# A linear-attention scan and a squared-ReLU FFN in one kernel: pairs of chunks, two tokens per partition, and an issue order written by hand

## The chip, the cores and the metric

One core of one Trainium2 chip. The metric is device microseconds of one launch, from the runtime's own clock; it runs about 2 us longer than the span of the profile, which goes from the first to the last instruction. A run is called slow when it is more than 1.5% above the fastest run of the same kernel.

Engines: PE is TensorE, PEld its weight loads, DVE VectorE, ACT ScalarE, POOL GpSimd, SP SyncE. A name with q behind it is that engine's instruction queue where it waits or issues a DMA.

## The reference

Four batches, 8 heads, 768 tokens, head size 32, state size 16. A selective scan with a scalar decay per head and token, in chunks, feeds a two-layer FFN over all 3072 tokens. In condensed form:

```python
cum = np.cumsum(log_a, axis=-1)                       # within a chunk
M = einsum('bhin,bhjn->bhij', C, B) * exp(cum_i - cum_j) * causal
y = einsum('bhij,bhjd->bhid', M, x) + einsum('bhin,bhnd->bhid', C, state) * exp(cum)
state = exp(sum(log_a)) * state + sum_j B_j x_j * exp(cum_last - cum_j)
...
x = y.transpose(0, 2, 1, 3).reshape(3072, 256)
h = np.maximum(x @ w_in, 0.0)                         # 256 -> 2048
out = h * h @ w_out                                   # 2048 -> 256
```

The reference uses chunks of 32 tokens. The length changes the order of the sums and not the result, so both kernels use 128.

## The kernel before

A unit is one batch and one chunk: 24 units. Each has transposes, two groups of four score matmuls, eight 128-column masks, the output and the state. The FFN works on blocks of 512 tokens. The issue order is left to a scheduler, and the score tiles and the FFN's first layer take buffers from one PSUM pool of four (`ps4`).

```python
        for hg in range(2):
            mtq = []
            for q in range(4):
                mt0 = ps4.tile([128, 128], FP32, tag="acc", padded_shape=[128, 512], ...)
                ...
                nc.tensor.matmul(mt0, lhsT, rhs, start=True, stop=True, tile_position=(32 * q, 0))
                mtq.append(mt0)
            mts4 = u_pool.tile([128, 512], BF16, tag="mts4")
            for q in range(4):
                nc.vector.tensor_tensor(out=mts4[:, q * 128:(q + 1) * 128], in0=mtq[q],
                                        in1=mask4[:, 0:128], op=ALU.mult)
...
        for f in range(4 * qi, 4 * qi + 4):               # FFN, a quarter of a 512-token block
            hps = ps4.tile([128, 512], FP32, tag="acc", name=f"hps_{f}")
            for kt in range(2):
                nc.tensor.matmul(hps, w_in_bf[kt][:, f * 128:(f + 1) * 128],
                                 T[:, kt, tb * 512:(tb + 1) * 512], start=(kt == 0), stop=(kt == 1))
            ...
            nc.scalar.activation(out=hbf, in_=hps, func=AF.Relu)
            nc.vector.tensor_tensor(out=h2t, in0=hbf, in1=hbf, op=ALU.mult)
...
        for k in range(2):                                # weights: 3 DMAs from SyncE
            nc.sync.dma_start(out=w_in_f[k], in_=moe_w_in[k * 128:(k + 1) * 128, :])
            nc.scalar.copy(out=w_in_bf[k], in_=w_in_f[k])
```

Of the kernel before, what the change touches and what calls it, by code (L numbers as in the profile page):

```python
# [10 lines left out]
FP32 = mybir.dt.float32  # L12
# [5 lines left out]
def _free_ap(base: bass.AP, offset_elems: int, free_dims):  # L18
    ap0 = list(base.ap)[0]
    return bass.AP(tensor=base.tensor, offset=base.offset + offset_elems,  # L20
                   ap=[list(ap0)] + [list(d) for d in free_dims])


@with_exitstack
def kernel(
# [9 lines left out]
):  # L35
    nc = tc.nc
    NB, NH, S, D = 4, 8, 768, 32
    NST = 16
    L = 128
    NC = S // L  # L40
    NTOK = NB * S

    const_pool = ctx.enter_context(tc.tile_pool(name="const", bufs=1))
    prep_pool = ctx.enter_context(tc.tile_pool(name="prep", bufs=1))
    w_pool = ctx.enter_context(tc.tile_pool(name="w", bufs=1))
    big_pool = ctx.enter_context(tc.tile_pool(name="big", bufs=1))
    bc_pool = ctx.enter_context(tc.tile_pool(name="bc", bufs=3))
    u_pool = ctx.enter_context(tc.tile_pool(name="u", bufs=2))
    st_pool = ctx.enter_context(tc.tile_pool(name="st", bufs=2))
    f_pool = ctx.enter_context(tc.tile_pool(name="f", bufs=2))  # L50
    h2_pool = ctx.enter_context(tc.tile_pool(name="h2", bufs=2))

    eye_bf_np = np.eye(128, dtype=np.float32).astype(ml_dtypes.bfloat16)
    triu_np = np.triu(np.ones((128, 128), dtype=np.float32))
    stril_np = (np.arange(128)[:, None] > np.arange(128)[None, :]).astype(np.float32)
    ones_np = np.ones((128, 128), dtype=np.float32)
    m = (np.arange(128)[:, None] <= np.arange(128)[None, :]).astype(np.float32)
    mask4_np = np.tile(m, (1, 4)).astype(ml_dtypes.bfloat16)

    eye_bf_d = nc.inline_tensor(eye_bf_np, name="eye_bf")  # L60
    eye32_d = nc.inline_tensor(np.eye(32, dtype=np.float32), name="eye32_f")
    dec_d = nc.inline_tensor(np.concatenate([triu_np, stril_np, ones_np], axis=1), name="dec_f32")
    mask4_d = nc.inline_tensor(mask4_np, name="mask4_bf")

    eye_bf = const_pool.tile([128, 128], BF16)
    eye32_f = const_pool.tile([32, 32], FP32)
    dec = const_pool.tile([128, 3, 128], FP32)
    mask4 = const_pool.tile([128, 512], BF16)
    zrow = const_pool.tile([1, 128], BF16)
    nc.sync.dma_start(out=eye_bf, in_=eye_bf_d.ap())  # L70
    nc.sync.dma_start(out=eye32_f, in_=eye32_d.ap())
    nc.sync.dma_start(out=dec, in_=dec_d.ap().rearrange("p (t c) -> p t c", t=3))
    nc.sync.dma_start(out=mask4, in_=mask4_d.ap())
    nc.vector.memset(zrow, 0.0)

    w_in_bf = [w_pool.tile([128, 2048], BF16, name=f"w_in_bf{k}") for k in range(2)]
    w_out_bf = w_pool.tile([128, 16 * 256], BF16)

    T = big_pool.tile([128, 2, NTOK], BF16)

    P_sb = prep_pool.tile([128, 192], FP32)
    Pinv_sb = prep_pool.tile([128, 192], FP32)
    Qrev_sb = prep_pool.tile([128, 192], FP32)
    plast_bd = prep_pool.tile([128, 48], FP32)

    with tc.tile_pool(name="prep2", bufs=1) as prep2, \
         tc.tile_pool(name="ps_prep", bufs=1, space=bass.MemoryType.PSUM) as ps_prep:
        a_nat = prep2.tile([32, S], FP32)
        la_nat = prep2.tile([32, S], FP32)
        la_T = prep2.tile([128, 192], FP32)  # L90
        nc.sync.dma_start(out=a_nat, in_=a.rearrange("b h s -> (b h) s"))
        nc.scalar.activation(out=la_nat, in_=a_nat, func=AF.Ln)
        for cc in range(NC):
            latr = ps_prep.tile([128, 32], FP32, name=f"latr{cc}", tag="latr", padded_shape=[128, 512])
            nc.tensor.transpose(latr, la_nat[:, cc * 128:(cc + 1) * 128], eye32_f)
            nc.vector.tensor_copy(out=la_T[:, cc * 32:(cc + 1) * 32], in_=latr)
        dps = [ps_prep.tile([128, 192], FP32, name=f"dps{t}", tag=f"dps{t}", padded_shape=[128, 512]) for t in range(3)]
        for t in range(3):
            nc.tensor.matmul(dps[t], dec[:, t, :], la_T, start=True, stop=True)
        nc.scalar.activation(out=P_sb, in_=dps[0], func=AF.Exp)  # L100
        nc.scalar.activation(out=Pinv_sb, in_=dps[0], func=AF.Exp, scale=-1.0)
        nc.scalar.activation(out=Qrev_sb, in_=dps[1], func=AF.Exp)
        ptot = prep2.tile([128, 192], FP32)
        nc.scalar.activation(out=ptot, in_=dps[2], func=AF.Exp)
        for q in range(4):
            src = _free_ap(ptot[32 * q:32 * (q + 1), 0:1], q, [[8, 4], [4, 2], [32, 6]])
            nc.vector.tensor_copy(
                out=plast_bd[32 * q:32 * (q + 1), :].rearrange("p (b g c) -> p b g c", b=4, g=2),
                in_=src)

    ps4 = ctx.enter_context(tc.tile_pool(name="ps4", bufs=4, space=bass.MemoryType.PSUM))
    ps_a = ctx.enter_context(tc.tile_pool(name="ps_a", bufs=1, space=bass.MemoryType.PSUM))

    def pad_cols(t):
        return _free_ap(t[:, 0:1], NST, [[32, 8], [1, NST]])

    state_prev = {}
    sps_g = ps_a.tile([128, 128], FP32, tag="sprime", padded_shape=[128, 512], name="sps_g")
    nc.tensor.matmul(sps_g, zrow, zrow, start=True, stop=True, skip_group_check=True)

    pref = {}

    def prefetch(u):
        if u >= NB * NC:
            return
        b, c = u // NC, u % NC
        x_nat = bc_pool.tile([128, 8, 32], FP32, tag="x_nat")
        B_nat = bc_pool.tile([128, 8, NST], FP32, tag="B_nat")
        C_nat = bc_pool.tile([128, 8, NST], FP32, tag="C_nat")
        sl = slice(c * 128, (c + 1) * 128)  # L130
        nc.sync.dma_start(out=x_nat, in_=x[b][:, sl, :].transpose([1, 0, 2]))  # L131
        nc.sync.dma_start(out=B_nat, in_=B[b][:, sl, :].transpose([1, 0, 2]))  # L132
        nc.sync.dma_start(out=C_nat, in_=C[b][:, sl, :].transpose([1, 0, 2]))  # L133
        pref[u] = (x_nat, B_nat, C_nat)

    def ssd_unit(b, c):
        u = b * NC + c
        col0 = c * 32 + b * 8
        x_nat, B_nat, C_nat = pref.pop(u)
        prefetch(u + 3)  # L140
        x4 = bc_pool.tile([128, 8, 32], BF16, tag="x4")
        nc.gpsimd.tensor_copy(out=x4, in_=x_nat)  # L142
        BPinv = bc_pool.tile([128, 256], BF16, tag="BPinv")
        CP = bc_pool.tile([128, 256], BF16, tag="CP")
        Bds = bc_pool.tile([128, 8, NST], BF16, tag="Bds")
        nc.gpsimd.memset(pad_cols(BPinv), 0.0)  # L146
        nc.gpsimd.memset(pad_cols(CP), 0.0)
        pinv_b = _free_ap(Pinv_sb[:, col0:col0 + 1], 0, [[1, 8], [0, NST]])
        p_b = _free_ap(P_sb[:, col0:col0 + 1], 0, [[1, 8], [0, NST]])
        qrev_b = _free_ap(Qrev_sb[:, col0:col0 + 1], 0, [[1, 8], [0, NST]])  # L150
        out_strided_B = _free_ap(BPinv[:, 0:1], 0, [[32, 8], [1, NST]])
        out_strided_C = _free_ap(CP[:, 0:1], 0, [[32, 8], [1, NST]])
        nc.gpsimd.tensor_tensor(out=out_strided_B, in0=B_nat, in1=pinv_b, op=ALU.mult)  # L153
        nc.gpsimd.tensor_tensor(out=out_strided_C, in0=C_nat, in1=p_b, op=ALU.mult)  # L154
        nc.vector.tensor_tensor(out=Bds, in0=B_nat, in1=qrev_b, op=ALU.mult)
        bct_ps = ps_a.tile([128, 512], BF16, tag="bct", padded_shape=[128, 1024])
        for gi, src_t in enumerate((BPinv, CP)):
            for hg in range(2):
                nc.tensor.transpose(bct_ps[:, (gi * 2 + hg) * 128:(gi * 2 + hg + 1) * 128],  # L159
                                    src_t[:, hg * 128:(hg + 1) * 128], eye_bf)  # L160
        bct = bc_pool.tile([128, 512], BF16, tag="bct_sb")
        nc.vector.tensor_copy(out=bct, in_=bct_ps)  # L162
        ypsum = ps_a.tile([128, 2, 128], FP32, tag="ypsum", padded_shape=[128, 2, 256])
        mts = {}
        for hg in range(2):
            mtq = []
            for q in range(4):
# [68 lines left out]
    for u0 in range(3):  # L236
        prefetch(u0)
# [10 lines left out]
    for tb in range(6):  # L248
        for qi in range(4):
            items.append(("q", tb, qi))  # L250
# [54 lines left out]
```

## Time and profile before

| | before |
|---|---|
| time, median of 3 runs | 200.64 us |
| span of the profiled run, granted TensorE clock | 197.0 us, 0.99 |
| TensorE busy | 86% of the span |
| first FFN matmul | 34.95 us |
| a block of 512 tokens, in the full part | 27.7 us |

The prediction below shows the busy row, the tenths and the timeline. Three rows of the costliest groups complete it. Their columns: line, engine, operation, output and inputs, shapes, count; then busy time and the mean ns of one; then the engine's idle time ahead of them and what ended most of it.

```profile
L219 ACT ACTIVATE hbf<-hps 128x512 bf16<-128x512 f32 x96 | 53.6, 596 | 25.9 <-PE hps L214 18.8
L175 DVE TENSOR_TENSOR mts<-mt,mask 128x128 bf16<-128x128 f32 x192 | 47.8, 286 | 26.6 <-PE mt L171 23.4
L171 PE MATMUL mt<-bct 32*128 32x128 bf16 x192 | 29.5, 233 | 2.6 <-ACT hbf L219 1.1
```

ACT and DVE wait for TensorE far longer (18.8 and 23.4 us) than TensorE waits ahead of the scores (2.6 us). TensorE's own stream of many small, separate groups is the limit.

### The profile page before, as it was taken

What the parts mean: (1) busy time and instruction counts of PE and PEld (TensorE: products, weight loads), DVE (VectorE), ACT (ScalarE), POOL (GpSimd) and SP (SyncE); (2) the same over time, 40 slices, a digit from 0 to 9 for tenths busy, and PEclk for the clock granted to TensorE, in tenths of its full rate; (3) what the DMA queues carried; (4) which work ended last, traced back from release to release, by engine and by line L of the source; (5) the groups of instructions that cost most, each with busy time, mean ns of one, the idle gap of its engine ahead of it and who ended that gap; (6) DMA issues with size and microseconds to landing.
All of it is one profiled execution on the core that took longest, in us unless ns stands there. A gap on an engine that the chain in (4) does not pass through costs nothing.

```text
span 197.0 us, 3713 instructions
## 1 busy us (share of the span) xinstructions
PE 169.6 (86%) x1290; PEld 92.9 (47%) x1301; DVE 113.5 (58%) x387; ACT 82.6 (42%) x154; POOL 37.3 (19%) x124
## 2 busy tenths in 40 slices
PE   0356667899999999999999999999999999889883
PEld 0243233344575444564445764446754446633462
DVE  0155657586656768538858367775568674346600
ACT  2420734638222836223664216291137452238710
POOL 2151125421233110215112050213230000000000
PEclk9999999999999999999999999999999999979999
DMA  4978997963156313248320637130400001100011
GB/s 111 116 106 318 370 218 83 114 74 40 26 103 104 44 13 40 47 91 114 42 34 1 105 84 79 13 45 27 93 32 0 0 0 44 57 9 0 3 53 53
DMA packets 81233, 14.32 MB, mean 73 GB/s; under 512 B 75552, under 2 KB 80928, under 8 KB 80960
## 3 DMA queue, kind: packets, MB, share of 16 engines
q1 hardware_dynamic: 81216, 14.10, 38.9%
q8 instruction: 10, 0.16, 0.4%
q14 instruction: 7, 0.06, 0.1%
HBM read 10.95 MB, written 3.15 MB: 72 GB/s over the span
## 4 chain that ended last, share of the span: by engine, by line
PE 68%; ACT 10%; DMA 8%; SPq 4%; issue 4%; DVE 4%; POOL 1%; ACTq 0%; POOLq 0%
PE ops L228 24%; PE hps L214 14%; PE ypsum L184 10%; PE mt L171 9%; ACT hbf L219 9%; DMA B_nat<-in_B_dram 7%; PE bct_ps L159 4%; PE sps_g L192 4%; PE ypsum L180 3%; SPq L133 1%; DMA x_nat<-in_x_dram 1%; SPq L131 1%; DVE bct L162 1%; SPq L132 1%; ACT osb L232 1%
## 5 line engine op out<-in xcount | busy, mean ns | idle before, releaser
L219 ACT ACTIVATE hbf<-hps 128x512 bf16<-128x512 f32 x96 | 53.6, 596 | 25.9 <-PE hps L214 18.8
L175 DVE TENSOR_TENSOR mts<-mt,mask 128x128 bf16<-128x128 f32 x192 | 47.8, 286 | 26.6 <-PE mt L171 23.4
L228 PE MATMUL ops<-w_out_bf,h 128*128 128x256 bf16 x384 | 55.4, 274 | 1.8 <-ACT osb L232 1.4
L220 DVE TENSOR_TENSOR h<-hbf 128x512 bf16<-128x512 bf16 x96 | 41.1, 428 | 21.3 <-ACT hbf L219 18.9
L214 PE MATMUL hps<-T,w_in_bf 128*128 128x512 bf16 x181 | 47.8, 399 | 2.5 <-ACT T L188 1.6
L228 PEld LDWEIGHTS <-h 128*128 128x128 bf16 x384 | 33.2, 97 | 9.8 <-issue 1.9
L184 PE MATMUL ypsum<-mts,x 128*32 128x128 bf16 x192 | 31.8, 239 | 1.2 <-issue 1.0
L171 PE MATMUL mt<-bct 32*128 32x128 bf16 x192 | 29.5, 233 | 2.6 <-ACT hbf L219 1.1
L214 PEld LDWEIGHTS <-w_in_bf 128*128 128x128 bf16 x192 | 18.9, 101 | 24.4 <-issue 7.6
L232 ACT COPY osb<-ops 128x256 f32<-128x256 f32 x24 | 8.9, 372 | 42.4 <-PE ops L228 42.4
L142 POOL CAST x<-x_nat 128x256 bf16<-128x256 f32 x24 | 10.2, 427 | 67.0 <-issue 23.5
L171 PEld LDWEIGHTS <-bct 32*128 32x128 bf16 x192 | 11.6, 92 | 20.9 <-issue 8.8
L188 ACT CAST T<-ypsum 128x256 bf16<-128x256 f32 x24 | 9.0, 373 | 28.1 <-PE ypsum L184 25.3
L184 PEld LDWEIGHTS <-x 128*32 128x32 bf16 x192 | 12.4, 94 | 16.6 <-issue 9.6
L202 DVE SCALAR_TENSOR_TENSOR state<-state,plast_bd,sps_g 128x128 bf16<-128x128 bf16 x32 | 11.0, 343 | 11.5 <-PE sps_g L192 7.0
L192 PE MATMUL sps_g<-x,Bds 128*16 128x32 bf16 x192 | 9.4, 184 | 4.2 <-DVE state L200 2.2
L146 POOL MEMSET BPinv<- 128x128 bf16 x24 | 4.9, 205 | 39.2 <-PE bct_ps L159 38.7
L180 PE MATMUL ypsum<-bct,state 128*128 128x128 bf16 x40 | 9.5, 237 | 1.9 <-ACT T L188 1.9
L162 DVE COPY bct<-bct_ps 128x512 bf16<-128x512 bf16 x24 | 10.0, 417 | 1.5 <-PE bct_ps L159 1.5
L153 POOL TENSOR_TENSOR BPinv<-B_nat,Pinv_sb 128x128 bf16<-128x128 f32 x24 | 9.8, 409 | 3.2 <-DMA B_nat<-in_B_dram 3.0
L154 POOL TENSOR_TENSOR CP<-C_nat,P_sb 128x128 bf16<-128x128 f32 x24 | 10.1, 420 | 1.6 <-DMA C_nat<-in_C_dram 1.0
L192 PEld LDWEIGHTS <-Bds 128*16 128x16 bf16 x192 | 4.8, 86 | 10.3 <-issue 4.9
(30 smaller groups left out, 65.6 us busy)
## 6 DMA issues: line engine op xcount, KB each, us to landing
x_nat<-in_x_dram SPq DMA_DIRECT2D x24, 128.0 KB, 2.8
out_dram<-osb SPq DMA_DIRECT2D x24, 128.0 KB, 1.8
w_in_f<-in_moe_w_in_dram SPq DMA_DIRECT2D x2, 1024.0 KB, 5.9
w_out_f<-in_moe_w_out_dram SPq DMA_DIRECT2D x1, 2048.0 KB, 12.8
B_nat<-in_B_dram SPq DMA_DIRECT2D x24, 64.0 KB, 2.9
C_nat<-in_C_dram SPq DMA_DIRECT2D x24, 64.0 KB, 2.6
dec<-dec_f SPq DMA_DIRECT2D x1, 192.0 KB, 2.4
mask<-mask_bf SPq DMA_DIRECT2D x1, 128.0 KB, 2.3
```

The lines of the kernel that those rows point to most:

```text
L162: nc.vector.tensor_copy(out=bct, in_=bct_ps)
L171: nc.tensor.matmul(mt0, lhsT, rhs, start=True, stop=True, tile_position=(32 * q, 0))
L175: nc.vector.tensor_tensor(out=mts4[:, q * 128:(q + 1) * 128], in0=mtq[q], in1=mask4[:, 0:128], op=ALU.mult)
L180: nc.tensor.matmul(ypsum[:, hg, :], state_prev[(b, hg)], bct[:, (2 + hg) * 128:(2 + hg + 1) * 128], start=(hg == 0), stop=False, skip_grou ...
L184: nc.tensor.matmul(ypsum[32 * q:32 * q + 32, hg, :], x4[:, hg * 4 + q, :], mts[hg][:, q * 128:(q + 1) * 128], start=(c == 0 and hg == 0), ...
L192: nc.tensor.matmul(sps[32 * q:32 * q + NST, 32 * q:32 * q + 32], Bds[:, hg * 4 + q, :], x4[:, hg * 4 + q, :], start=True, stop=True, skip_ ...
L202: nc.vector.scalar_tensor_tensor(out=st_new, in0=state_prev[(b, hg)], scalar=plast_bd[:, uu:uu + 1], in1=sps, op0=ALU.mult, op1=ALU.add)
L214: nc.tensor.matmul(hps, w_in_bf[kt][:, f * 128:(f + 1) * 128], T[:, kt, tb * 512:(tb + 1) * 512], start=(kt == 0), stop=(kt == 1))
L219: nc.scalar.activation(out=hbf, in_=hps, func=AF.Relu)
L220: nc.vector.tensor_tensor(out=h2t, in0=hbf, in1=hbf, op=ALU.mult)
L228: nc.tensor.matmul(ops, h2[f][:, tt * 128:(tt + 1) * 128], w_out_bf[:, f * 256:(f + 1) * 256], start=(f == 0), stop=(f == 15))
L232: nc.scalar.copy(out=osb, in_=ops)
```

## The change

Its intent: fewer and larger groups. A pair is one chunk of two batches at once (12 pairs); a partition holds two neighbouring tokens, so an input DMA moves runs twice as long; the FFN has 256-token blocks, in 96 steps of four first-layer and four second-layer matmuls; the order of each engine is written out instead of scheduled. Transposes, scores and outputs of a pair share one four-bank PSUM buffer (tag "A", one buffer). The weights come in five pieces, 45 DMAs in all, from ACT's queue. The core of it, with cuts marked:

```diff
-        mt0 = ps4.tile([128, 128], FP32, tag="acc", ...)            # one per head
-        nc.vector.tensor_tensor(out=mts4[:, q * 128:(q + 1) * 128], in0=mtq[q], ...)
+    mt = ps_s.tile([128, 4, 2, 2, 128], FP32, tag="A", name=f"mt{k}")
+    def ph_mask(k, q):                                              # 512 columns at once
+        nc.vector.tensor_tensor(out=v["mts"][:, q], in0=v["mt"][:, q], ...)
 ...
+    def load_w(f0, f1):
+        for g in range(2):
+            for q in range(4):
+                nc.scalar.dma_start(
+                    out=w_in_f[32 * q:32 * q + 32, g, f0 * 128:f1 * 128],
+                    in_=moe_w_in[q * 64 + g * 32:q * 64 + g * 32 + 32, f0 * 128:f1 * 128])
+        nc.scalar.dma_start(out=w_out_f[:, f0:f1, :], in_=...)
 ...
+        for k in range(2, NPAIR):
+            s0 = 8 * k - LEAD
+            at(s0 - 4, ph_prep, k, ...)
+            at(s0, ph_tr, k)                      # transposes, copy bct
+            at(s0 + 1, ph_mt, k)                  # scores
+            for q in range(4):
+                at(s0 + 2 + q, ph_mask, k, q)     # masks, one per step
+            at(s0 + 6, ph_y, k)                   # outputs and state matmuls
+            at(s0 + 7, ph_T, k)                   # T copy on ACT
+            at(s0 + 7, ph_state, k)               # state update on DVE
+        for s in range(len(steps) + LAG):
+            if s < len(steps):
+                mm1(*steps[s])                    # 4 matmuls, ReLU on ACT, square on DVE
+            for fn, args in todo.pop(s, []):
+                fn(*args)
+            if s >= LAG:
+                mm2(*steps[s - LAG])              # 4 matmuls
```

So in a step each engine meets the FFN's part first, then the pair's phase, then the second layer.

Names used below: `tr` is a pair's transposes and `bct` their copy in SBUF, `mt` the scores and `mts` the masked scores, `Y` the outputs (with the new states), `T` their copy for the FFN, `z` the first half of the state update; mm1 and mm2 are the FFN's two layers. In the prediction SSD is the scan, a drain is time that TensorE loses when the tile shape of its matmuls changes, and a lane wait is a wait for one of the DMA semaphores.

## The prediction

> **What bounds the kernel now.** I read the busy row first, then the chain that ended last, then the timeline of TensorE in a stretch where it never rests.
>
> ```profile
> PE 169.6 (86%) x1290; PEld 92.9 (47%) x1301; DVE 113.5 (58%) x387; ACT 82.6 (42%) x154; POOL 37.3 (19%) x124
> ...
> PE   0356667899999999999999999999999999889883
> ...
> PE 68%; ACT 10%; DMA 8%; SPq 4%; issue 4%; DVE 4%; POOL 1%; ACTq 0%; POOLq 0%
> ```
>
> TensorE is the bound: 68% of the chain, nine tenths busy from slice 8 on. Before that lie some 35 us of start: the timeline has the first FFN matmul at 34.95 us, after four of the 24 SSD units. What fills the busy part:
>
> ```profile
> 141.29 1.91 PE L228 MATMUL ops<-w_out_bf,h 128*128 128x256 bf16 x16
> ...
> 140.72 0.23 PE L171 MATMUL mt<-bct 32*128 32x128 bf16 x4
> 140.89 0.24 PE L184 MATMUL ypsum<-mts,x 128*32 128x128 bf16 x4
> 141.06 0.28 PE L159 MATMUL bct_ps<-eye_bf,CP 128*128 128x128 bf16 x2
> ...
> 144.69 0.23 PE L184 MATMUL ypsum<-mts,x 128*32 128x128 bf16 x1
> 144.85 0.23 PE L171 MATMUL mt<-bct 32*128 32x128 bf16 x1
> 145.01 0.23 PE L184 MATMUL ypsum<-mts,x 128*32 128x128 bf16 x1
> 145.17 0.22 PE L171 MATMUL mt<-bct 32*128 32x128 bf16 x1
> ```
>
> Read the start times. Four row-tiled mt matmuls take 0.17 us until the next kind starts; one alone takes 0.16 us. So a group of one costs what a group of four costs, and the scheduler makes many groups of one, because each mt waits for a PSUM buffer that ACT or DVE frees one at a time. FFN matmuls run at (1.91-0.27)/15 = 0.11 us per 256 columns, 0.216 per 512. The state matmul that follows a chunk recurs at 62.94, 91.38, 118.93 and 146.03: a 512-token block takes 27.7 us. FFN work in it: 32 x 0.216 + 64 x 0.11 = 14.0 us of TensorE, so half of the block is SSD matmuls and waits. One more loss: a run of ReLUs paces mm1 at 0.575 us per 512x128 tile (x8 in 4.54) where its two matmuls need 0.43.
>
> **What the Trainium skill says.** "TensorEngine Tiling (Array Packing)", Key Properties: changing the tiling mode drains TensorE. The trace agrees: 0.16 us between starts in alternation, against 0.11 for a 256-column matmul. "TensorE: Matmul & The Clock Gate", Part 3, says matmuls on different tiles start some 4 ns apart. The trace fits: eight state matmuls of one mode (171.58) show 0.22 us, four 0.19. "VectorE: DVE Perf Modes", the perf-mode tier table: tensor_tensor with a PSUM operand runs at 1x. Its 0.96 GHz gives 1.04 ns per element; the trace's 128-column mask recurs every (1.84-0.28)/7 = 0.22 us, which leaves a fixed 0.09. No page prices DMA issue in this pattern; the SyncE rows do, below.
>
> **The change, part by part.** FFN: the same columns, 96 steps of four mm1 and four mm2 matmuls of 256 columns, 8 x 0.11 = 0.88 us a step. Nothing is gained per column. ACT has one 128x512 ReLU per step (0.596) and DVE one square (0.428, recurring after 0.34), both under 0.88, so the ReLU pace no longer binds.
>
> SSD per pair (two old units), now four unbroken phases. Transposes 6 x 0.06 + 0.1 = 0.47 us. Scores: 16 tiled matmuls of 256 columns on 8 tile positions, four rounds of 0.11 plus a drain, 0.6. Y phase: 16 + 16 + 32 tiled matmuls; rounds of four or eight at 0.05 to 0.08 plus three drains of about 0.1, 1.5 us (guess 1.1 to 2.2). With eight steps: 7.04 + 0.47 + 0.6 + 1.5 = 9.6 us per pair, against 13.8 for half a block now. If nothing waited, ten pairs would win 42 us.
>
> But transposes, scores and Y share ONE four-bank PSUM buffer, and the issue order shows one wait in front of each phase. Count from the start of step s0's mm1:
> (a) scores wait for the bct copy, which is queued on DVE behind the square of s0. mm1 ends 0.44, ReLU 0.64 to 1.24, square 1.3 to 1.64, copy (0.417 for 512 bf16, so 0.55 for 768) ends 2.25. TensorE is there at 1.88. Stall 0.37.
> (b) Y waits for all four masks. One 512-column mask costs 0.22 + 384 x 1.04 ns = 0.62 us, and each stands behind a square: 0.34 + 0.62 = 0.96 per step on DVE against 0.88 on TensorE. The first pair begins at about 4.6, the fourth ends at 8.45; TensorE arrives at 7.25. Stall 1.2.
> (c) the next transposes wait for the T copy on ACT and z on DVE, both behind the ReLU and square of step s0+7: mm1 ends, +0.2 +0.6 +0.34 +0.35, about 1.5 us, while TensorE has 0.88 us of work. Stall 0.65.
> Sum 2.2 us, so 11.8 us per pair: half of the gain is given back to the single buffer.
>
> Start: weights are now fetched by 45 DMAs issued from ACT's own queue, in ACT's order. SyncE's rows give the price of an issue:
>
> ```profile
> 2.05 0.43 SPq L73 DMA_DIRECT2D mask<-mask_bf  x1
> 2.53 0.45 SPq L91 DMA_DIRECT2D a_nat<-in_a_dram  x1
> 3.02 0.43 SPq L131 DMA_DIRECT2D x_nat<-in_x_dram  x1
> ```
>
> Each recurs after about 0.45 us. Before the first T copy ACT must issue 27, before the second all 45: 45 x 0.45 = 20 us of ACT's sequencer. P is ready at 6.4 us (a lands near 4 us, clamp, two scans, transposes, copy), nine DMAs and the B cast to 11, then 36 x 0.45 = 16.2, two weight casts (1.2) and copies (1.3), perhaps 1 us of waits for one of eight DMA semaphores: the first ReLU at 30.5 us. The data themselves would be there sooner: 4 MB of weights at the 370 GB/s that the page shows is 11 us. So the start shortens by only some 4 us.
>
> Sum. Start 30.5; six steps before pair 2 with the late weight casts on ACT 5.3 + 1.2; ten pairs x 11.8 = 118; the last ten steps and three mm2 8.8 + 1.3; tail 4.6 (0.2 drain, 0.6 copy of 128x512, four output issues 1.8, landing 1.8). 169.7 us of span. Before, the time was 200.64 for a span of 197.0, 3.6 more. 173.3 us. POOL (some 3 us of work per pair) and input DMA (half the packets, since two tokens are contiguous) stay beside.
>
> **Rivals.**
> R1, waits are hidden and TensorE alone sets the pace: 9.6 us per pair gives 151 us. For it: DVE and ACT total about 6.7 and 6.0 us per pair, well below. Against it: the single buffer's order above; average load does not say when a copy finishes.
> R2, the waits compound: the Y phase takes 2.2 us since matmuls on one bank may queue, DVE falls behind on squares, TensorE cools. The trace has a sample of cooling: in 174.7 to 178.3, after three us of mostly small SSD matmuls, the granted clock was 0.53 and a 512-column matmul took 0.43 us. 14 us per pair gives 195 us, near the old time.
> R3, the start: if ACT's issues cost 0.1 us rather than 0.45, the first ReLU comes near 26 us, bound by the serial SSD of two pairs, and the time is 169; if lane waits dominate, issues take 0.6 and the time is 180.
>
> **Range and chances.** R1 cannot be full, since (b) follows from durations in the table; half of it gives 162. R2 in part gives 185. I add 4 us either way for R3. 173, range 158 to 189. A loss would need 14 us per pair and a slow start at once. Faster by over 2% (below 196.6) 0.93, same 0.05, slower 0.02.
>
> **What would show it.** Steps: first ReLU between 27 and 34 us, with ACT's queue full of DMA issues before it. Period of the Y phase 11.8 us (between 10.5 and 13). In each period TensorE idle ahead of the first Y matmul with DVE's mask as releaser, near 1.2 us; ahead of the scores with the bct copy, 0.4; ahead of the transposes with T or z, 0.6. Mask 0.69 us busy, ReLU still 0.6. TensorE still first on the chain, DVE's share up from 4%. Wrong if: the period is below 10.5 (phases packed better or no waits), or above 13 with a granted clock well below 1, or the start is above 36 us.

## The result, and the profile after

The changed kernel takes 173.94 us (median of four runs, 173.16 to 176.54, the last one slow), beside 201.25 us for the kernel before in the same rounds. The ratio is 0.869, with a 95% interval of 0.8603 to 0.8777. Ratios here are the mean time of one kernel's fast runs over that of the other's of the same rounds, so not quite the ratio of the medians quoted. Outputs are correct. The profiled run took 173.16 us, with a span of 171.4.

From the page of the changed kernel: busy row, TensorE's tenths, the chain that ended last by engine and by line, then three groups.

```profile
PE 111.3 (65%) x1740; PEld 89.5 (52%) x1740; DVE 85.8 (50%) x182; ACT 72.6 (42%) x129; POOL 32.0 (19%) x46
...
PE   0132012304976896968958869689685897979970
...
PE 32%; DVE 28%; DMA 17%; ACT 10%; issue 5%; SPq 2%; ACTq 2%; DVEq 0%
...
L278 ACT ACTIVATE hb<-hps 128x512 bf16<-128x512 f32 x96 | 57.5, 602 | 56.6 <-PE hps L275 56.4
...
L196 DVE TENSOR_TENSOR mts<-mt,cb 128x512 bf16<-128x512 f32 x48 | 32.2, 682 | 2.2 <-PE mt L185 2.2
...
L213 PE MATMUL Y<-bct,S 32*32 32x128 bf16 x160 | 4.0, 216 | 13.7 <-DVE mts L196 13.7
```

TensorE is busy 111.3 us instead of 169.6, but for only 65% of the span: its tenths are never a run of nines again, and none of the first nine slices, up to 38 us, is above three tenths. The chain is shared between PE (32%) and DVE (28%). The last row gives the largest wait of the steady part: 13.7 us of TensorE idle ahead of the first output matmul of a pair, all ended by DVE's masks.

TensorE's timeline over one pair (start and duration in us first; in brackets the idle time before, and what ended it) shows three waits of the shared buffer:

```profile
79.86 0.22 PE L166 MATMUL tr<-cb,Bb 128*128 128x128 bf16 x1 [0.61 <-DVE z L263]
...
81.72 0.44 PE L185 MATMUL mt<-bct 32*64 32x256 bf16 x16 [0.49 <-DVE bct L171]
82.10 0.61 PE L290 MATMUL ops<-w_out_b,h 128*128 128x256 bf16 x4
...
88.36 0.40 PE L213 MATMUL Y<-bct,S 32*32 32x128 bf16 x16 [1.72 <-DVE mts L196]
88.69 0.25 PE L224 MATMUL Y<-xs,Bb 64*32 64x64 bf16 x16
...
89.22 0.61 PE L290 MATMUL ops<-w_out_b,h 128*128 128x256 bf16 x4
```

The wait ahead of the scores is an exception. In seven of the ten the scores start as in the next one, 0.53 us after the first-layer matmuls ahead of them, where such a group takes 0.44 if nothing waits:

```profile
92.52 0.60 PE L275 MATMUL hps<-T,w_in_b 128*128 128x256 bf16 x4
93.05 0.44 PE L185 MATMUL mt<-bct 32*64 32x256 bf16 x16
```

A bracket counts from the modelled end of the last matmul, 0.60 us after its group's start instead of 0.44, so it understates a wait by 0.16 us. By start times a pair loses, on average over the nine periods, 1.52 us ahead of the outputs, 0.74 ahead of the transposes and 0.17 ahead of the scores.

The output phase, start to the next kind's start, is 89.22 - 88.36 = 0.86 us, the scores 82.10 - 81.72 = 0.38. The outputs of the ten pairs begin at 54.86 for the first and at 153.72 us for the last, so a period is 98.86 / 9 = 10.98 us.

The start, on ACT and its queue:

```profile
5.23 4.38 ACTq L129 DMA_DIRECT2D w_in_f<-in_moe_w_in_dram  x8
...
16.02 7.23 ACTq L129 DMA_DIRECT2D w_in_f<-in_moe_w_in_dram  x8
...
24.75 8.85 ACTq L129 DMA_DIRECT2D w_in_f<-in_moe_w_in_dram  x7
...
34.20 5.46 ACTq L129 DMA_DIRECT2D w_in_f<-in_moe_w_in_dram  x8
...
40.17 0.58 ACT L247 CAST T<-Y 128x512 bf16<-128x512 f32 x1 [5.38 <-DMA w_in_f<-in_moe_w_in_dram]
40.65 0.60 ACT L278 ACTIVATE hb<-hps 128x512 bf16<-128x512 f32 x1
```

Eight issues take 4.4 to 7.2 us and seven even 8.85. All 45 add up to 33.9 us, 0.75 each. But the issues alone are only 21.0 us of that, summed from the trace's single records; the median of the 40 for w_in is 0.432 us. The other 12.9 us lie between them and are nearly all waits (an issue that waits for nothing follows the last after 0.04 us). The T copy of the second pair stands behind the last of them and waits 5.38 us, and the first ReLU starts at 40.65 us, later than the first FFN matmul of the kernel before (34.95). What holds an issue is in the chain of that stretch (start, duration, what):

```profile
24.62 6.33 DMA x_nat<-in_x_dram
...
30.97 1.68 ACTq L129
...
33.17 0.43 ACTq L129
...
33.64 4.73 DMA w_out_f<-in_moe_w_out_dram
...
38.40 1.78 DMA w_in_f<-in_moe_w_in_dram
40.18 0.58 ACT T L247
```

An issue on ACT at 30.97 was released by the landing of x_nat, a DMA that SyncE had issued. The trace's records of the issues name eight semaphores, which both queues use in turn, and each of the 45 weight issues waits for the one that it then uses itself. So issues wait for earlier DMAs of either queue to land, and what stands behind a waiting issue waits too.

Where the 25.6 us of span went:

| | before | after | change |
|---|---|---|---|
| to the first FFN matmul (before) or first ReLU (after) | 34.95 | 40.65 | +5.7 |
| from there to the last second-layer matmul | 158.8 | 125.3 | -33.5 |
| tail | 3.3 | 5.5 | +2.2 |

The first landmarks are not quite the same thing. The first FFN matmuls of the changed kernel ran at 30.55 us; their ReLU then waited ten microseconds for ACT, and TensorE with it (9.22 us idle). Twice as many output DMAs (48), four of them behind the last copy, go with the longer tail.

### The profile page after: what moved, and what is told of

Read it like the earlier page. It is cut to its first block, busy times and chain, and to the rows that moved or that the text cites. A ratio compares the mean times of both kernels' runs of the same rounds, so it can differ in the third digit from the quotient of the medians.

```text
span 171.4 us, 4268 instructions
## 1 busy us (share of the span) xinstructions
PE 111.3 (65%) x1740; PEld 89.5 (52%) x1740; DVE 85.8 (50%) x182; ACT 72.6 (42%) x129; POOL 32.0 (19%) x46
## 4 chain that ended last, share of the span: by engine, by line
PE 32%; DVE 28%; DMA 17%; ACT 10%; issue 5%; SPq 2%; ACTq 2%; DVEq 0%
DVE mts L196 13%; PE ops L290 12%; DVE h L280 11%; PE hps L275 10%; DMA x_nat<-in_x_dram 6%; ACT hb L278 5%; ACT T L247 3%; DMA w_out_f<-in_moe_w_out_dram 3%; DMA w_in_f<-in_moe_w_in_dram 3%; DMA C_nat<-in_C_dram 3%; PE Y L213 2%; PE mt L185 2%; SPq L119 2%; PE Y L234 2%; DMA B_nat<-in_B_dram 2%
## 5 line engine op out<-in xcount | busy, mean ns | idle before, releaser
L278 ACT ACTIVATE hb<-hps 128x512 bf16<-128x512 f32 x96 | 57.5, 602 | 56.6 <-PE hps L275 56.4
L280 DVE TENSOR_TENSOR h<-hb 128x512 bf16<-128x512 bf16 x96 | 45.7, 477 | 47.5 <-ACT hb L278 47.5
L275 PE MATMUL hps<-T,w_in_b 128*128 128x256 bf16 x384 | 59.0, 278 | 9.2 <-ACT T L247 9.2
L290 PE MATMUL ops<-w_out_b,h 128*128 128x256 bf16 x384 | 57.4, 273 | 0.0
L275 PEld LDWEIGHTS <-w_in_b 128*128 128x128 bf16 x384 | 38.1, 99 | 14.9 <-issue 9.7
L196 DVE TENSOR_TENSOR mts<-mt,cb 128x512 bf16<-128x512 f32 x48 | 32.2, 682 | 2.2 <-PE mt L185 2.2
L144 POOL TENSOR_TENSOR cz<-C_nat,P_sb 128x256 bf16<-128x256 f32 x11 | 7.9, 717 | 57.9 <-DMA C_nat<-in_C_dram 50.7
L156 POOL TENSOR_TENSOR xs<-x_nat,Pinv 128x512 bf16<-128x512 f32 x12 | 13.7, 1141 | 14.0 <-DMA x_nat<-in_x_dram 12.8
L213 PE MATMUL Y<-bct,S 32*32 32x128 bf16 x160 | 4.0, 216 | 13.7 <-DVE mts L196 13.7
L247 ACT CAST T<-Y 128x512 bf16<-128x512 f32 x12 | 7.0, 582 | 5.4 <-DMA w_in_f<-in_moe_w_in_dram 5.4
L295 ACT COPY osb<-ops 128x512 f32<-128x512 f32 x12 | 7.0, 583 | 1.2 <-PE ops L290 1.2
```

The source lines that it names most:

```text
L144: e_c.tensor_tensor(out=_fap(czk, 0, [[144, 4], [32, 4], [1, 16]]), in0=_fap(t["C"][:, 0, :], 0, [[16, 4], [64, 4], [1, 16]]), in1=_fap(P_ ...
L156: e_x.tensor_tensor(out=_fap(xs[:, 0, :], 0, [[256, 2], [32, 8], [1, 32]]), in0=_fap(t["x"][:, 0, :], 0, [[32, 2], [64, 8], [1, 32]]), in1 ...
L196: nc.vector.tensor_tensor(out=v["mts"][:, q], in0=v["mt"][:, q], in1=_fap(cb[:, 128:129], 0, [[128, 2], [0, 2], [1, 128]]), op=ALU.mult)
L213: nc.tensor.matmul(Y[32 * q:32 * q + 32, u, g * 128:(g + 1) * 128], S_b[32 * q:32 * q + 32, u, g * 32:(g + 1) * 32], ct_ap(v["bct"], q, g, u),
L247: nc.scalar.copy(out=_fap(t[:, 0, :], 0, [[128, 2], [256, 2], [1, 128]]), in_=Y[:, 0:2, 0:256].rearrange("p u (g i) -> p u g i", g=2))
L275: nc.tensor.matmul(hps[:, j, :], w_in_b[:, g, f * 128:(f + 1) * 128], T[blk][:, g, :], start=(g == 0), stop=(g == 1), skip_group_check=True)
```

## The experiments

Theory: in the steady part each pair loses some 2 us to waits of the one shared buffer, of which that for the masks is the largest; in the start ACT's in-order queue is held by DMA issues. Rivals: TensorE's own order or drains set the period (then moving work on DVE gains nothing); the start is bound by the bytes or by landing, not by who issues. All kernels below give correct results. The first four ran together, then the next four, then the last three, each group with its own runs of the kernel before. Means below are of fast runs; the changed kernel's is 173.68 us (three). Between the groups the kernel before moved by about 1 us (170.99 / 0.8535 = 200.3, 140.30 / 0.7044 = 199.2), so gains across groups are no better known than that.

### T copy and state update one step sooner

```diff
-            at(s0 + 7, ph_T, k)
-            at(s0 + 7, ph_state, k)
+            at(s0 + 6, ph_T, k)
+            at(s0 + 6, ph_state, k)
```

> The copy of Y to T and the state update stand one step earlier in the issue order (right behind the Y phase instead of behind the ReLU and the square of the next step). Theory (the single four-bank buffer makes the phases wait in turn): the wait of about 0.6 us ahead of the transposes, seen in eight of ten pairs of the changed kernel, goes, and what is saved stays saved: 10 x 0.6 = 6 us, so about 168 us, Y phases 10.4 us apart instead of 11.0. Rival (the chain of squares and masks on DVE sets the period whatever the transposes do): the wait moves to the Y phase, whose wait for the masks grows from 1.4 to about 2 us, and the time stays at 174.

Measured: 171.32 us median, ratio 0.8535 (0.8462 to 0.8608), mean 170.99: 2.7 us gained, under 2%, and the interval just touches that of the changed kernel. The period fell from 10.98 to 10.64 us, with 10.4 expected. TensorE's timeline of one pair in this kernel:

```profile
78.78 0.22 PE L166 MATMUL tr<-cb,Bb 128*128 128x128 bf16 x1
...
80.56 0.44 PE L185 MATMUL mt<-bct 32*64 32x256 bf16 x16 [0.40 <-DVE bct L171]
```

The wait of 0.61 us ahead of the transposes is gone, and a wait of 0.4 stands ahead of the scores in nearly every pair (5.9 us in all; of the 2.1 before, only 0.49 lay behind the third pair). The copy of the transposes on DVE still stands behind the same square, so transposes that come sooner mostly wait there. The mechanism holds; the gain is less than half of what was expected because one wait hid the other.

### Masks one step sooner

```diff
-                at(s0 + 2 + q, ph_mask, k, q)
+                at(s0 + 1 + q, ph_mask, k, q)
```

> Each of the four masks stands one step earlier in DVE's order. Theory: Y then waits for a mask that ends about one step (0.9 us) sooner; worked from the trace's durations the wait ahead of Y falls from 1.4 to about 0.3 us, ten times: 163 us (161 to 166), Y phases about 9.9 us apart. Rival (DVE is saturated in these steps, square 0.34 + mask 0.62 against 0.88 us of TensorE): squares come late instead, TensorE waits ahead of mm2 or mm1, and less than 3 us is won, 171 or more.

Measured: 163.01 us, ratio 0.813 (0.8065 to 0.8195), mean 162.88: 10.8 us gained. The wait ahead of the outputs fell from 13.7 to 2.7 us in all, and the period to 9.88 us. In the pair shown, one of four, the outputs now start without a wait (the other six wait 0.16 to 1.07 us), and the transposes keep theirs:

```profile
83.74 0.40 PE L213 MATMUL Y<-bct,S 32*32 32x128 bf16 x16
...
87.13 0.22 PE L166 MATMUL tr<-cb,Bb 128*128 128x128 bf16 x1 [0.62 <-DVE z L263]
```

No instruction was added or taken away; only DVE's order changed. This was the largest single loss of the steady part.

### Both

The two edits above together.

> Both edits. Theory: the two waits are at different places of the period and add up: 6 + 11 us, 157 us (155 to 161), Y phases 9.3 us apart, near the 8.6 us that the trace's own TensorE starts sum to without waits. Rival: only one of the two counts, as DVE's chain binds; not below 163.

Measured: 160.21 us, ratio 0.7988 (0.7921 to 0.8056), mean 160.04: 13.6 us gained, about the sum of 2.7 and 10.8. The period is 9.53 us. The wait of 0.4 us ahead of the scores stays in nearly every pair (5.7 us in all), which would explain why it did not reach 157; a run below takes it away.

### The output phase broken up by FFN matmuls

The four second-layer matmuls of the step were put between the phase's parts:

```diff
+                break_y()                  # behind each batch's 8 state matmuls
...
+                if r == 0:
+                    break_y()              # twice within the 32 intra matmuls
```

> The step's four FFN matmuls stand between the four groups of state matmuls of the Y phase, one behind each group of four, instead of behind the whole phase; same instructions, same waits. Theory (what the change gains on TensorE is that tiled matmuls run in unbroken phases): each excursion costs what the trace of the kernel before shows, 0.16 us for a tiled group and 0.22 for a lone FFN matmul that a tiled one follows, so 4 x 0.38 = 1.52 against 0.33 + 0.44 = 0.77 unbroken: +0.75 us per pair, +7 us in all, about 181 us. Rival (the mixing cost nothing, the gain came from elsewhere, the ReLU pace or the single waits of the mt buffers): within 1.5 us of 174.

One correction to that text: it speaks of four groups of state matmuls. As built, and as the trace shows, one FFN matmul stood behind each of the two halves of the state matmuls and two within the intra-chunk matmuls. So there were four breaks, but not at the places named. Measured: 183.4 us, ratio 0.9104 (0.9008 to 0.9199), mean 182.92: 9.2 us lost. The trace of this kernel:

```profile
66.96 0.29 PE L213 MATMUL Y<-bct,S 32*32 32x128 bf16 x8 [1.08 <-DVE mts L196]
67.19 0.28 PE L303 MATMUL ops<-w_out_b,h 128*128 128x256 bf16 x1
67.40 0.29 PE L213 MATMUL Y<-bct,S 32*32 32x128 bf16 x8
```

A lone 256-column matmul between tiled ones occupies 67.40 - 67.19 = 0.21 us, where four in a row take 0.44. From the first output matmul to the first-layer matmuls behind it took 68.92 - 66.96 = 1.96 us, against 66.84 - 65.54 = 1.30 in the changed kernel: 0.66 us in six of the ten pairs and more in the others, so at least 6.6 in ten, or 0.16 per break. That is what unbroken phases save, tested by itself. The other 3 us or so go with a lower granted clock (0.954 to 0.977 in the four runs, 0.981 to 0.995 in the changed kernel's): 0.57 at 93 to 96 us, 0.82 at 102 to 108 and 0.81 at 126 to 132, where the changed kernel had 1.00 in the same stretches. Why the clock fell stays open: the wait ahead of the phase was no longer than in the changed kernel (12.9 against 13.7 us in all).

### 25 weight DMAs instead of 45, still on ACT

```diff
-        for g in range(2):
-            for q in range(4):
-                nc.scalar.dma_start(
-                    out=w_in_f[32 * q:32 * q + 32, g, f0 * 128:f1 * 128], ...)
+        for q in range(4):
+            nc.scalar.dma_start(
+                out=w_in_f[32 * q:32 * q + 32, :, f0 * 128:f1 * 128], ...)
```

> Only the start is changed: each piece of w_in is fetched by four DMAs instead of eight (both halves of 32 rows in one), so ACT issues 25 weight DMAs instead of 45, with the same bytes and the same runs in memory. Three theories of why the first ReLU comes at 40.6 us. A (the prediction's: issue time on ACT's sequencer, 0.45 us each): 20 x 0.45 = 9 us sooner, about 31.5 us, 165 us in all. B (each DMA waits until the eighth before it, of either queue, has landed, as the order of waits and the chain show; 33.9 us of ACT's queue for 45 is 0.75 each): up to 15 us sooner, but not before the serial work of two pairs, 27 to 29 us; 160 to 163 us in all. C (the DMA engines are simply full, 0.5 to 0.9 busy): no change, 173 to 175.

Measured: 169.15 us, ratio 0.8432 (0.8345 to 0.852), mean 168.46: 5.2 us gained. First ReLU at 35.62. None of the three theories had 5. The trace of this kernel:

```profile
20.70 7.37 ACTq L128 DMA_DIRECT2D w_in_f<-in_moe_w_in_dram  x4
...
35.14 0.58 ACT L247 CAST T<-Y 128x512 bf16<-128x512 f32 x1 [4.90 <-DMA w_in_f<-in_moe_w_in_dram]
```

Four issues took 7.37 us, 1.8 each, and the median issue alone 0.334: this time is mostly waits for landings, and with fewer issues each waits longer. So the number of DMAs is not the whole price, and neither is it nothing.

### The same 45 DMAs from SyncE

```diff
-                nc.scalar.dma_start(
+                nc.sync.dma_start(
                     out=w_in_f[32 * q:32 * q + 32, g, f0 * 128:f1 * 128],
```

(and the same for w_out)

> The same 45 weight DMAs in the same places of the program, but issued from SyncE's queue instead of ACT's. A (ACT's sequencer time is what costs): ACT copies T as soon as Y is there, the first ReLU comes near 26 us, the later weight casts wait for SyncE, which now issues some 65 DMAs one after the other (0.45 to 0.65 us each), so that the last weights land near 42 us; the time falls by 4 to 8 us to 166 to 170. B (the eight semaphores set the pace, whichever queue issues): the first ReLU may come sooner, but the weights and the loads of pairs 1 to 3 come no sooner than before, and the time stays within 3 us of 174.

Measured: 163.2 us, ratio 0.8169 (0.8081 to 0.8258), mean 162.98: 10.7 us gained, more than either theory gave. The trace of this kernel, first SyncE's queue:

```profile
5.80 3.87 SPq L129 DMA_DIRECT2D w_in_f<-in_moe_w_in_dram  x8
```

and ACT at the second T copy and the first ReLU:

```profile
21.50 0.59 ACT L247 CAST T<-Y 128x512 bf16<-128x512 f32 x1 [1.38 <-PE Y L234]
22.44 0.60 ACT L278 ACTIVATE hb<-hps 128x512 bf16<-128x512 f32 x1 [0.35 <-PE hps L275]
```

Bytes, DMAs and sizes are the same; only the issuing engine differs, and with it the queue. Eight issues take 3.87 us, 0.48 each, and the second T copy waits for TensorE, not for a DMA. By the records SyncE's 45 issues take 20.5 us, about as long as ACT's 21.0, but only one of them waits for a landing (0.25 us). So two things changed at once: ACT is free of the issues, and the waits for landings are nearly gone. No run separates them. The first ReLU comes 18.2 us sooner. Of that some 7.5 us are lost again: the casts of the later pieces now wait for their weights (1.06 us for the third and 4.69 for the fourth), and the scores of the third pair wait 4.38 us for their transposes' copy. After that wait the granted clock was 0.55 (36 to 40 us).

### Transposes one place sooner still

On top of both steady edits, the transposes are issued behind the second layer of the step before, ahead of the next step's square on DVE.

```diff
-            at(s0, ph_tr, k)
+            post.setdefault(s0 - 1, []).append(k)
...
                 mm2(*steps[s - LAG])
+            for k in post.pop(s, []):
+                ph_tr(k)
```

> As the run with both edits (masks and T one step earlier; 160.2 us), and the transposes stand at the end of the step before, so that their copy on DVE is ahead of the next square. In that run the wait of 0.4 us ahead of the scores for this copy was the last regular one of the period (9.5 us). Theory: it goes, the period falls to 9.1, the time to 156. Rival: the transposes then wait for the state update (z ends 0.2 us before they could start) or the masks come later, and nothing is won: 160.

Measured: 154.09 us, ratio 0.7701 (0.7636 to 0.7765), mean 153.84: 6.2 us below the version without it. TensorE's wait for the transposes' copy fell from 5.7 to 0.7 us. The profiled run is one marked slow (155.99 us, clock 0.996); its period is 9.03 us.

### That order with 25 DMAs on ACT

> The edits of the start (25 weight DMAs) and of the order (masks, T and transposes earlier) together. The start and the steady part follow one another, so the gains should add up: whatever the first wins against 174 and the second wins against 174, taken from 174; by theory B and the removal of the third wait 174 - 12 - 18 = 144 us (142 to 150). Rival: with the loop starting sooner, the weights of the later columns or the loads of pairs 2 and 3 come too late for it, and part of the start's gain turns into waits in the first steps: above 150.

Measured: 150.18 us, ratio 0.7511 (0.7455 to 0.7566), mean 150.05: 3.8 us gained and just outside the range expected. The first ReLU is at 35.62 again, as in the run with 25 DMAs alone. I had counted on 12 us from the start before that run was seen.

### 25 weight DMAs from SyncE

The two edits of the start together.

> The changed kernel with its weights fetched by 25 DMAs (both halves of w_in in one) issued from SyncE, so that ACT issues only the two constants. It completes a square: 45 on ACT 173.9 us, 25 on ACT 169.2, 45 on SyncE 163.2. Theory A (with ACT free, what is left of the start is the length of SyncE's queue at 0.48 us per issue): the 20 issues fewer bring the third weight piece forward by some 16 x 0.48 = 7.7 us, the wait of 4.69 us ahead of its cast goes, and about a third of the 3 us wait behind it: first ReLU at 20 to 21.5 us, 155 to 159 us in all. Theory C (the casts wait for the bytes, not for their issue): casts as late as with 45, 161.5 to 163.5 us. Theory D (a DMA of two halves takes so much longer that it lands no sooner): first ReLU not before 22.4 and the time 162 to 166.

Measured: 160.36 us median of four runs, two of them slow; the two fast ones, 158.66 and 158.93, are too few for an interval. Their mean is 4.2 us below that with 45. First ReLU at 20.89. So the count does cost when SyncE issues, at the weak end of Theory A. The cast of the fourth piece (the expectation calls it the third) still waited 4.32 us. Its issues began only at 24.84 us, behind two of C_nat that took 3.40 us and two of x_nat that took 2.68, where 1.31 is usual. The records show no wait for a landing there: the issues themselves took longer, while the DMA engines were 0.92 to 0.94 busy (17 to 25 us). That speaks for a part of Theory C and does not show it.

### That order with 45, and with 25, from SyncE

> The 45 weight DMAs on SyncE, with the SSD order of tr_early (masks one step sooner, T copy and state update one step sooner, transposes at the end of the step before). If the start and the period are independent terms, the gains add: 163.2 - (173.9 - 154.1) = 143.4 us, expected 142 to 146, first ReLU near 22.4, period near 9.05. If the late loads of pairs 2 and 3 behind the weights hold an order that wants them sooner, 146 to 150, with waits of PE ahead of the transposes or scores of pairs 2 and 3.

Measured: 144.92 us median; three of the four runs were slow, the fast one took 142.54 us. First ReLU at 22.97. The gains of start and steady part add, as far as one fast run can say.

> As best2 with 25 weight DMAs instead of 45. If Theory A of sp_fewer holds, its 5 to 8 us come off as well: 136 to 140 us, first ReLU at 20 to 21.5, period near 9.05. If Theory C holds, the same as best2 within 1 us. This is the version that should beat both kernels, by 30% against the kernel before.

Measured: 140.73 us, ratio 0.7044 (0.6981 to 0.7107), mean 140.30. The median is just above the range expected. First ReLU at 21.00. The gaps between the outputs of neighbouring pairs are 10.75 us once, then (120.16 - 47.95) / 8 = 9.03. The first gap lies where the page shows a granted clock of five tenths in one slice. TensorE over most of a period of this kernel:

```profile
75.25 0.40 PE L213 MATMUL Y<-bct,S 32*32 32x128 bf16 x16
...
76.10 0.61 PE L290 MATMUL ops<-w_out_b,h 128*128 128x256 bf16 x4
...
77.42 0.22 PE L166 MATMUL tr<-cb,Bb 128*128 128x128 bf16 x1
...
79.16 0.44 PE L185 MATMUL mt<-bct 32*64 32x256 bf16 x16
```

In this pair the brackets are gone from all three phases; in five of the ten the outputs still wait 0.27 to 0.48 us for the masks. This version is 19% below the changed kernel (140.30 / 173.68, of different rounds) and 29.6% below the one before.

## Why the prediction was right, and where it was wrong

The total, 173.3 against 173.16 us in the profiled run, was right by luck: two errors of about 10 us cancelled. Its terms against the trace:

| | predicted | measured | error |
|---|---|---|---|
| to the first ReLU | 30.5 | 40.65 | +10.2 |
| first ReLU to last second-layer matmul | 134.6 | 125.3 | -9.3 |
| tail | 4.6 | 5.5 | +0.9 |
| time above the span | 3.6 | 1.8 | -1.8 |

The last line was a slip: it set a median beside the span of one profiled run. In the later runs, which list both, time and span differ by 1.8 to 1.9 us in either kernel.

**TensorE as the bound, and its relief.** Right. A step took 0.87 us (0.88 predicted) and the ReLU, 0.602 us, no longer paces it. Breaking one phase at four places cost at least 6.6 us of TensorE's time, so it is shown that unbroken phases save time. What share of the 33.5 us they make is not shown: no run tests the ReLU pace, or the scores' single PSUM buffers, by itself.

**The step that failed: "perhaps 1 us of waits for one of eight DMA semaphores".** The term beside it, "45 x 0.45 = 20 us of ACT's sequencer", held: the 45 issues alone took 21.0 us. But ACT's queue lost another 12.9 us between them, nearly all of it in waits for landings, which covers the 10.2 us by which the first ReLU came late. I took the price of an issue from SyncE's rows at the beginning of the kernel before, where no earlier DMA had to land first, so they said nothing of these waits. The mechanism, compute held behind issues, was right and the size of the waits was wrong. Rival R3 named lane waits, 0.6 us an issue in all; it was the true one and still too mild (0.75). By the experiments, moving the issues off ACT is worth 10.7 us, with the waits that end by it; how many issues there are is worth 5.2 us on ACT and 4.2 on SyncE; and the data are not what the first FFN step lacks, since its ReLU could start at 22.44 us with the same DMAs. In the changed kernel itself the first FFN matmuls ran at 30.55 us, the very time predicted for the ReLU; the ten microseconds behind them are ACT, held by its issues. The Trainium skill says in "DMA: Bandwidth & Descriptors", section "Issuing engines are not separate DMA queues", that starting DMAs on several engines saves only the sequencer's own time for it, "which is usually small relative to the DMA itself". Here that saving was negative: two issuing engines were 10.7 us slower than one, with compute behind one engine's issues and waits between them.

**The step that was mis-sized: the period, 11.8 us, measured 10.98.** The output phase was guessed at 1.5 us (1.1 to 2.2) and took 0.86, outside the guess: by start times 16 state matmuls 0.33, 16 update matmuls 0.07, 32 intra-chunk matmuls 0.46. The 0.07 flatters the update: in the last two pairs, which have none, the phase takes 0.68, so it costs 0.17. I had charged three drains of 0.1. By the single records one is there, 0.135 us from the last state matmul to the first update, but the update and the intra-chunk matmuls have the same tile shape, 64*32, and follow within 0.005. Scores took 0.38 (predicted 0.6), transposes 0.33 (0.47). That is 8.5 us of pure work with the steps instead of 9.6.

**The three waits.** (b), the masks: predicted 1.2 us, idle 1.05 to 1.88, mean 1.37; confirmed by moving the masks, which gave 10.8 us. One mask took 0.682 us busy as against 0.69 predicted; beside the 0.286 of a 128-column one that is 1.03 ns a column, and the prediction had 1.04. (c), the transposes: predicted 0.65, idle 0.61 in eight of ten pairs. (a), the scores: predicted 0.37, and hardly there: 0.09 us in seven of the ten pairs. The prediction counted (a) and (c) from the same step as if both were paid. But while TensorE waits for z, (c), the square ahead of the copy of the transposes gets done, so (c) hides (a). Taking (c) away alone brought (a) out, 0.4 us of idle time a pair, and gave 2.7 of 6 us. By start times the waits sum to 2.4 us; with 8.5 they make 10.9 of the 10.98. So the sum of the waits, predicted 2.2, came right with two waits instead of three.

**The rivals.** R1 (151 us, nothing waits) was wrong for this order, but the order by hand could be made so: 153.84 us with the start untouched. R2 (waits compound, TensorE cools) did not occur in the changed kernel, which kept a clock of 0.995; its cooling did occur when the phase was broken up. The range held, and "faster by over 2%" was right. By its own tests the prediction was wrong in two points, "the start is above 36 us" and the wait of 0.4 ahead of the scores "in each period", and right in the period between 10.5 and 13, the mask as releaser and DVE's share of the chain (28%, from 4%).

A few of its readings do not come out as written, none by enough to matter: the parts of the tail sum to 4.4 and not 4.6; x8 in 4.54 gives a ReLU pace of (4.54 - 0.60) / 7 = 0.56 and not 0.575; three groups of FFN matmuls and the transposes bring TensorE to the scores at 1.79 and not 1.88; and what stands at 91.38 in the kernel before are transposes, not a state matmul.

## What to carry to other kernels

With one shared buffer, count for every phase which engine's queue its releaser stands in and behind what; moving four masks by one place in DVE's order was worth 10.8 us and cost nothing. Issue DMAs from an engine that has no compute to do at that time: a DMA issue can wait for earlier landings, and everything behind it in the queue waits too. A predicted total that agrees proves little: compare its terms with the trace.

## What the Trainium skill lacked or had wrong

- "DMA: Bandwidth & Descriptors", section "Anatomy of one DMA — SWDGE (gpsimd) path", puts sequencer dispatch at some 50 ns, which is GpSimd's path. For SyncE and ACT the skill is not silent, as the prediction's "No page prices DMA issue in this pattern" suggests: the same page, in a table of section "Why a DMA increments its semaphore by 16 and not by 1", gives 512 sequencer cycles for one DMA in "previous generations", without a time and without naming trn2. The runs show 0.42 to 0.63 us on SyncE where nothing holds an issue, and a median of 0.432 on ACT. No page says what a queue loses between issues: here 12.9 us in 45. That the wait is on the issuing sequencer, as the first section says, agrees with the 5.38 us ahead of the T copy.
- "TensorEngine Tiling (Array Packing)", Key Properties, gives no size for the drain on a mode change. Four excursions to an untiled matmul cost 0.66 us per pair, 0.16 each; from the last 32*32 matmul to the first 64*32 one it is 0.135 us between starts.
- "TensorE: Matmul & The Clock Gate", Part 3: some 4 ns from tile to tile fits the starts within the output phase (2 to 4 ns from one tile to the next in the records of one pair's state matmuls). It does not cover the return to a tile used just before: there the starts are 14 to 45 ns apart, and 16 state matmuls on four tiles took 0.33 us. Part 1 ties a low clock to idle windows; in the run with the broken phase it fell to 0.57 (93 to 96 us) although the longest idle time just before was 1.83 us, about as long as in the changed kernel (1.88), which kept 1.00. The cause stays open.
